# An attention, Fourier and MLP kernel: the MLP in thirds of a batch, with the residual added in place

## The chip, the cores and the metric

The kernel runs on one core of one Trainium2 chip. The metric is the device time of one execution in microseconds (us), with all inputs and outputs in HBM; runs of one kernel on one chip are compared with each other. Five engines work side by side, each through its own list of instructions in order: PE (matrix products), DVE (vector operations), ACT (activations and copies), POOL (a slower general engine) and SP (which here only issues DMAs). An instruction that waits holds up everything behind it on its own engine.

## What is computed

Four batches of 768 rows; q, k and v have 8 heads of 64, so a row has 512 values after attention. In numpy, cut to what matters:

```python
# attention: each chunk of 32 queries sees 16 keys to the left, its own 32, 8 to the right, 8 memory keys
a = np.exp(scale * q_c @ k_full.T - max); a = a / a.sum()
x[:, chunk] = a @ v_full                       # then heads side by side: (4, 768, 512)

mixed = np.real(np.fft.fft(np.fft.fft(x, axis=1), axis=2))
u = x + mixed
un = (u - u.mean(-1)) / np.sqrt(u.var(-1) + 1e-06)
ch = np.maximum(un @ w_ch1, 0.0) @ w_ch2       # 512 -> 2048 -> 512
return u + ch                                  # (4, 768, 512) float32
```

The last three lines are where the change lies: layer 1 (`w_ch1`) with its ReLU, layer 2 (`w_ch2`), and the residual `u`.

## The kernel before

**Rows and tiles.** A batch is six tiles of 128 rows. `xs[b]` (tile `xsb`, 128x6x512 float32, three buffers for four batches) holds a batch from the end of its attention on: first `x`, later `u`, written over it.

**Attention.** Heads go in pairs; pair n (0 to 15, four for each batch) loads q and k by POOL's DMAs and v by SP's (`e_load_v`, L350: seven DMAs, two of 220 KB among them, into buffer `va` n mod 4, so pair n + 4 loads into the buffer that pair n reads). PE turns q and k (batch 3's are turned by SP's DMAs instead), makes scores (`sc`), ACT takes their exponentials (`e`), PE multiplies them with the values (`xa`, `xo`, L455), and DVE divides into `xs[b]` (L465, L466).

**Fourier.** DVE folds the rows (`zy`, `pq`, `ff`), splits them into a high and a low half in 16 bits (`hi` by ACT, `lo` by DVE), PE multiplies by sine and cosine tables (`ps`, 193 columns wide), ACT and DVE split the result (`up`), and PE multiplies along the other axis (`e_columns`, L695: eight matmuls with 256 moving columns, each with its own stationary operand). The lower three tiles of a batch are got from the upper ones, with rows mirrored through HBM (`x_rows`, `x_back`, `xr`).

**Normalisation.** Tile by tile, in the order 0, 1, 3, 4, 2, 5 (batch 0: 0 to 5), DVE makes `u` (L701 or L585), its statistics (L709, L710), and ACT writes `un` = mean - u in float16 (L715). The scale by the deviation is left to the end, since ReLU lets a positive factor through. Then `un` is turned into `unT`: by PE and a DVE copy in batch 0, and in batches 1 to 3 by a DMA transpose from SP's queue, `e_flip` (L724), called a flip below. `SLOT` gives a tile its place in `unT`: places 0 to 5 hold tiles 0, 3, 4, 5, 1, 2.

**MLP.** `mlp` (L1172) takes a half of a batch at a time, 384 rows (three places). Layer 1 is 16 groups (`e_ch1`, L752) of four matmuls with 384 moving columns; after each, ACT's ReLU (`e_relu`, L759) writes a 128x384 slice of `hT`. Layer 2 (`e_ch2`, L766) makes each tile of 128 rows by 16 matmuls with 512 moving columns; DVE multiplies by `rstd` and adds `u` into a new tile `osb` (L795, four buffers), and a DMA stores `osb`: directly, or for mirrored rows by way of HBM (`out_rows`). The last tile of batch 3 goes in two halves of 256 columns (L773, L779, L787).

**What sets the order.** The class `Plan` simulates the engines with costs written in the code and emits the instructions in the order that comes out. The MLP's matmuls have the lowest rank: PE takes them when nothing else is ready in the plan. In its rows, `take` and `give` are buffers that a step needs and frees. Once the program is built the order is fixed, and each engine waits at its next instruction. PSUM has four banks (`mlp`, `acc`) that layer 1, layer 2, the Fourier products and the second half of the values share.

Of the kernel before, what the change touches and what calls it, by code (L numbers as in the profile page):

```python
# [177 lines left out]
def kernel(  # L178
# [47 lines left out]
    def let_go(t):  # L226
        for name, held in bank_of.items():
            for h in held:
                if h[0] is t:
# [15 lines left out]
    TURNED = 3  # L245
    cp_q = "p h j d -> p h (j d)"
# [4 lines left out]
                     xsb=3, fold=2, hl=1, up=4, dn=1, acc=2, mlp=2, un=6, unT=2, hT=1, osb=4))  # L251
# [5 lines left out]
    mkf = fpool.tile([P, 2, D], FP32, tag="osb", bufs=4, name="mkf")  # L257
    mkb = fpool.tile([P, 2 * D], BF16, tag="osb", bufs=4, name="mkb")
# [5 lines left out]
    yS = fpool.tile([P, 3, 2, NK], FP32, tag="unT", bufs=2, name="yS")  # L264
    rS = fpool.tile([P, 3, 2, NK], FP32, tag="unT", bufs=2, name="rS")
# [4 lines left out]
    ident = fpool.tile([P, P], FP32, tag="osb", bufs=4, name="ident")  # L270
# [204 lines left out]
    mu_of, unT_of, rstd_of, g_of = {}, {}, {}, {}  # L475
# [115 lines left out]
    def g_zy(par, g):  # L591
        if g == 0:
            zy_of[0, par] = fpool.tile([P, NST, P], FP32, tag="unT", bufs=2, name="zy0")
        xb, sl = xs[0], slice(3 * g, 3 * g + 3)
        nc.vector.tensor_tensor(zy_of[0, par][:, sl], xb[:, sl, 0:P], xb[:, sl, HD:HD + P],
                                ALU.add if par == 0 else ALU.subtract)
# [115 lines left out]
    def e_un(b, kt):  # L712
        un_of[b, kt] = un = fpool.tile([P, DM], FP16, tag="un", bufs=6, name="un")

        nc.scalar.activation(un, xs[b][:, kt, :], AFT.Identity, bias=mu_of[b][:, kt, 0:1],  # L715
                             scale=-1.0)
# [6 lines left out]

    def e_flip(b, kt):  # L724
        if kt == 0:
            unT_of[b] = fpool.tile([P, NDT, S], FP16, tag="unT", bufs=2, name="unT")
        nc.sync.dma_start_transpose(unT_of[b][:, :, ts(SLOT.index(kt), P)], un_of.pop((b, kt)))

    def e_unT(b, kt):
        if kt == 0:  # L730
            unT_of[b] = fpool.tile([P, NDT, S], FP16, tag="unT", bufs=2, name="unT")
        tp = tp_of.pop((b, kt))
        nc.vector.tensor_copy(unT_of[b][:, :, ts(kt, P)], tp)
        let_go(tp)

    def e_rstd(b):
        rstd_of[b] = rstd = fpool.tile([P, NST], FP32, tag="rstd", bufs=2, name="rstd")
        nc.gpsimd.tensor_scalar(rstd, mu_of[b][:, :, 1], eps, None, ALU.add)
        nc.gpsimd.tensor_tensor(rstd, rstd, mhalf, ALU.pow)

# [9 lines left out]
    ph_of, pc_of, hT_of, osb_of = ({} for _ in range(4))  # L750

    def e_ch1(b, sh, ht):  # L752
        ph_of[b, sh, ht] = ph = bank(pick(b, sh, ht)["tag"], [P, 512], FP32, "ph")
        for dt in range(NDT):
            nc.tensor.matmul(ph[:, 0:384], w1_sb[:, dt, ts(ht, P)],  # L755
                             unT_of[b][:, dt, sh * 384:(sh + 1) * 384],
                             start=(dt == 0), stop=(dt == NDT - 1))

    def e_relu(b, sh, ht):  # L759
        if ht == 0:  # L760
            hT_of[b, sh] = fpool.tile([P, NHT, 384], FP16, tag="hT", bufs=1, name="hT")
        ph = ph_of.pop((b, sh, ht))
        nc.scalar.activation(hT_of[b, sh][:, ht, :], ph[:, 0:384], AFT.Relu, bias=0.0, scale=-1.0)  # L763
        let_go(ph)

    def e_ch2(b, sh, stl, part):  # L766
        if part == 0:
            pc_of[b, sh, stl] = bank(pick(b, sh, stl, 0)["tag"], [P, DM], FP32, "pc")
        for ht in range(4 * part, 4 * part + 4):
            nc.tensor.matmul(pc_of[b, sh, stl], hT_of[b, sh][:, ht, ts(stl, P)], w2_sb[:, ht, :],  # L770
                             start=(ht == 0), stop=(ht == NHT - 1))

    def e_ch2_half(b, sh, stl, half):  # L773
        pc_of[b, sh, stl, half] = pc = bank(pick(b, sh, stl, 1 + half)["tag"], [P, HD], FP32, "pc")
        for ht in range(NHT):
            nc.tensor.matmul(pc, hT_of[b, sh][:, ht, ts(stl, P)], w2_sb[:, ht, ts(half, HD)],
                             start=(ht == 0), stop=(ht == NHT - 1))

    def e_osb_half(b, sh, stl, half):  # L779
        st, cols = slot(b, sh * 3 + stl), ts(half, HD)  # L780
        osb_of[b, st, half] = osb = fpool.tile([P, HD], FP32, tag="osb", bufs=4, name="osb")
        pc = pc_of.pop((b, sh, stl, half))
        nc.vector.scalar_tensor_tensor(osb, pc, rstd_of[b][:, st:st + 1], xs[b][:, st, cols],
                                       ALU.mult, ALU.add)
        let_go(pc)

    def e_out_half(b, st, half):  # L787
        (nc.sync, nc.scalar)[half].dma_start(out[b, ts(st, P), ts(half, HD)],
                                             osb_of.pop((b, st, half)))

    def e_osb(b, sh, stl):
        st = slot(b, sh * 3 + stl)
        osb_of[b, st] = osb = fpool.tile([P, DM], FP32, tag="osb", bufs=4, name="osb")
        pc = pc_of.pop((b, sh, stl))
        nc.vector.scalar_tensor_tensor(osb, pc, rstd_of[b][:, st:st + 1], xs[b][:, st, :],  # L795
                                       ALU.mult, ALU.add)
        let_go(pc)

    def e_out(b, st):
        (nc.scalar if b == B - 1 else nc.sync).dma_start(out[b, ts(st, P), :], osb_of.pop((b, st)))  # L800

    def e_out_rows(b, st):
        nc.sync.dma_start(od[b % 2, st - 3], osb_of.pop((b, st)))
# [200 lines left out]
    def weights(n):  # L1004
# [5 lines left out]
        else:  # L1010
            t_w2.extend(add("POOL", 0.7, lambda g=g: nc.gpsimd.dma_start(
                w2_sb[:, ts(g, 4), :], w2v[:, ts(g, 4), :]), moved=2.6, late=2.0,
                behind=t_ck[n], rank=t_ck[n]["rank"] + 0.1) for g in range(4))

    def first_fourier():
        t_rest, t_mid, t_row, pre = {}, {}, {}, {}
        for g in range(2):
            for par in range(2):
                zy = add("DVE", 0.5, lambda par=par, g=g: g_zy(par, g),
                         [t_norm[0, g], t_norm[1, g], t_sines],  # L1020
                         take=("unT",) if g == 0 else ())
# [7 lines left out]
                for ab in range(2):  # L1029
# [3 lines left out]
                                          take=("fold",) if (ab, g) == (0, 0) else (),  # L1033
                                          give=("unT",) if (ab, g) == (1, 1) else ())
# [12 lines left out]
            for par in range(2):  # L1047
                for ab in range(2):
# [5 lines left out]
                    else:  # L1054
                        ff = add("DVE", 0.55, lambda par=par, ab=ab: g_both(par, ab),
                                 pre[par, ab, 1][:2], give=("unT",) if ab == 1 else ())
# [59 lines left out]
    def columns_of(b, t_rest):  # L1116
        t_dn, t_un, cols = {}, {}, {}
        allr = list(t_rest.values())
        kts, sa = (0, 1, 2, 3, 4, 5), None
        if b == 0:  # L1120
# [21 lines left out]
        for i, kt in enumerate(kts):  # L1142
# [12 lines left out]
            sa = add("DVE", 0.9, lambda kt=kt: e_stats(b, kt), [su, sa])  # L1155
            un = add("ACT", 0.72, lambda kt=kt: e_un(b, kt), [sa], take=("un",))
            if b > 0:
                t_un[kt] = add("SP", 1.2, lambda kt=kt: e_flip(b, kt),
                               [un], behind=t_un.get(kts[i - 1]) if i else None,
                               take=("unT",) if i == 0 else (), give=("un",), late=2.5,  # L1160
                               loose=True)
                continue
# [3 lines left out]
                           take=("unT",) if kt == 0 else (), give=("mlp",))  # L1166
        rs = add("POOL", 1.0, lambda: e_rstd(b), [sa])
        return t_un, rs

    mlp_prev = [None]  # L1170

    def mlp(b, t_un, rs):  # L1172
        for sh in range(2):
            relu = []
            c2 = None
            for ht in range(NHT):
                ph = add("PE", 0.65, lambda sh=sh, ht=ht: e_ch1(b, sh, ht),
                         mlp_prev + [t_un[slot(b, 3 * sh + i)] for i in range(3)] + t_w1,
                         pick=pick(b, sh, ht), give=("unT",) if sh == 1 and ht == NHT - 1 else (),
                         rank=MLPS + len(plan.tasks), filler=True)  # L1180
                relu.append(add("ACT", 0.5, lambda sh=sh, ht=ht: e_relu(b, sh, ht),
                                [ph, relu[-1] if relu else None],
                                take=("hT",) if ht == 0 else (), give=(pick(b, sh, ht),),
                                rank=RELU(len(plan.tasks))))
            for stl in range(3):
                st, end_b = slot(b, 3 * sh + stl), 3 * sh + stl == NST - 1
                if end_b and b == B - 1:
                    for half in range(2):
                        c2 = add("PE", 1.76, lambda sh=sh, stl=stl, half=half:
                                 e_ch2_half(b, sh, stl, half), [relu[-1], t_w2[3], c2],  # L1190
                                 pick=pick(b, sh, stl, 1 + half), rank=MLPS + len(plan.tasks))
                        os_ = add("DVE", 0.4, lambda sh=sh, stl=stl, half=half:
                                  e_osb_half(b, sh, stl, half), [c2, rs], take=("osb",),
                                  give=(pick(b, sh, stl, 1 + half),))
                        add(("SP", "ACT")[half], 0.5, lambda st=st, half=half:
                            e_out_half(b, st, half), [os_], give=("osb",), moved=0.5)
                    continue
# [71 lines left out]
```

## Time and profile before

| What | Value |
|---|---|
| three timed runs | 284.81, 285.5, 283.14 us; median 284.81 |
| profiled execution, its own time from first to last instruction | span 284.2 us; the page gives nothing outside the span |
| granted PE clock | 1.000 |
| layer 1 matmul, 128x384, x512 | 86.7 us busy, 326 ns each (pipelined: the next starts before it ends) |
| layer 2 matmul, 128x512, x368 | 85.4 us busy, 380 ns each |
| ReLU on ACT, 128x384, x128 | 61.1 us busy, 492 ns each |
| `un` on ACT, 128x512, x24 | 17.3 us busy, 719 ns each |
| residual on DVE, 128x512, x23 | 17.2 us busy, 749 ns each |
| PE idle for the flip of batch 1 (`ph` waits for `unT`) | 1.5 us, once |

Busy times of PE overlap, so the time that a group of matmuls takes is read from the starts of consecutive groups, not from the mean of one. "L755" is line 755 of the kernel before; `ph` is layer 1's PSUM tile, `pc` layer 2's, `pm` that of `e_columns`.

### The profile page before, as it was taken

How to read it: one execution, taken by the hardware profiler on the slowest of the kernel's cores; microseconds unless marked ns; L12 is line 12 of the kernel's file. 1: busy time of each engine (PE TensorE's matmuls, PEld its weight loads, DVE VectorE, ACT ScalarE, POOL GpSimd, SP SyncE). 2: the span in 40 equal slices, each digit the busy share in tenths (PEclk: the TensorE clock that was granted, in tenths of full speed). 3: DMA queues.
4: the chain of work that ended last, by engine and by line, in shares of the span. 5: the costliest groups of instructions: out<-in, count | busy, mean ns of one | idle time of the engine just before them, and what ended most of it. 6: DMA issues, size and time to landing. Idle time of an engine off the chain costs nothing.

```text
span 284.2 us, 7142 instructions
## 1 busy us (share of the span) xinstructions
PE 267.9 (94%) x2941; PEld 170.7 (60%) x2941; DVE 164.4 (58%) x348; ACT 158.6 (56%) x294; POOL 58.3 (21%) x107
## 2 busy tenths in 40 slices
PE   0599999999999999998999999999999999999994
PEld 0476798765666766655667555657665545645644
DVE  7968979960348973897886960497669112012012
ACT  6887666588576575655952387228424822712700
POOL 8842652240210093441001020010000200000000
PEclk9999999999999999999999999999999999999999
DMA  6999999999899999999989963339304534004204
GB/s 102 202 168 167 194 204 204 197 197 192 134 199 271 145 233 156 140 155 211 154 180 113 205 158 64 78 149 148 113 0 111 140 83 110 4 37 111 39 37 111
DMA packets 116112, 39.92 MB, mean 140 GB/s; under 512 B 104560, under 2 KB 111472, under 8 KB 116080
## 3 DMA queue, kind: packets, MB, share of 16 engines
q1 hardware_dynamic: 93888, 23.54, 47.1%
q0 software_dynamic: 21472, 15.21, 34.0%
q10 hardware_dynamic: 720, 0.72, 0.8%
q8 instruction: 23, 0.38, 0.6%
q14 instruction: 9, 0.07, 0.1%
HBM read 37.36 MB, written 13.37 MB: 178 GB/s over the span
## 4 chain that ended last, share of the span: by engine, by line
PE 81%; DMA 11%; DVE 3%; SPq 1%; issue 1%; ACT 0%; POOL 0%; POOLq 0%; DVEq 0%
PE ph L755 30%; PE pc L770 27%; PE ps L527 6%; DMA va<-in_v_dram 5%; PE pm L695 4%; PE xa L455 3%; PE ps L684 3%; PE xo L455 3%; DMA va<-in_mem_v_dram 2%; PE sc L431 2%; DMA qs<-in_q_dram 2%; DMA unT<-un 2%; PE trq L375 1%; PE trk L375 1%; DVE xsb L701 1%; DVE st L709 1%
## 5 line engine op out<-in xcount | busy, mean ns | idle before, releaser
L755 PE MATMUL ph<-unT,w_sb 128*128 128x384 f16 x512 | 86.7, 326 | 1.5 <-DMA unT<-un 1.5
L763 ACT ACTIVATE hT<-ph 128x384 f16<-128x384 f32 x128 | 61.1, 492 | 47.8 <-PE ph L755 46.4
L770 PE MATMUL pc<-w_sb,hT 128*128 128x512 f16 x368 | 85.4, 380 | 0.0
L755 PEld LDWEIGHTS <-w_sb 128*128 128x128 f16 x512 | 49.2, 98 | 33.9 <-issue 1.9
L770 PEld LDWEIGHTS <-hT 128*128 128x128 f16 x368 | 34.1, 98 | 38.0 <-issue 0.7
L795 DVE SCALAR_TENSOR_TENSOR osb<-pc,rstd,xsb 128x512 f32<-128x512 f32 x23 | 17.2, 749 | 63.7 <-PE pc L770 63.7
L439 ACT ACTIVATE e<-sc,mbias 128x384 f32<-128x384 f32 x64 | 33.6, 577 | 16.2 <-PE sc L431 16.2
L715 ACT ACTIVATE un<-xsb,mu_s 128x512 f16<-128x512 f32 x24 | 17.3, 719 | 17.8 <-DVE mu_s L710 17.7
L539 ACT CAST up<-ps 128x386 f16<-128x386 f32 x16 | 9.6, 602 | 16.0 <-PE ps L527 15.5
L709 DVE BATCH_NORM_STATS2 st<-xsb 128x6 f32<-128x512 f32 x24 | 16.5, 689 | 0.6
L544 DVE TENSOR_TENSOR up<-ps,up 128x386 f16<-128x386 f32 x16 | 9.6, 600 | 11.6 <-ACT up L539 11.4
L517 DVE TENSOR_TENSOR lo<-ff,hi 128x768 f16<-128x768 f32 x12 | 11.5, 958 | 8.0 <-ACT hi L512 7.8
L455 PE MATMUL xa<-va,e 128*64 128x65 f32 x384 | 15.4, 232 | 0.0
L455 PEld LDWEIGHTS xa<-va,e 128*64 128x64 f32 x384 | 13.2, 143 | 3.4 <-issue 2.6
L455 PE MATMUL xo<-va,e 128*64 128x65 f32 x384 | 14.1, 223 | 0.0
L431 PEld LDWEIGHTS <-kTb 64*128 64x128 bf16 x384 | 7.8, 97 | 9.0 <-issue 7.3
L393 ACT COPY qT<-trq 128x768 bf16<-128x768 bf16 x12 | 9.5, 793 | 6.3 <-PE trq L375 6.3
L455 PEld LDWEIGHTS xo<-va,e 128*64 128x64 f32 x384 | 12.6, 138 | 0.4 <-ACT kTb L406 0.3
L570 POOL DMA_DIRECT2D xr<-x_back x3 | 2.3, 768 | 50.7 <-DMA x_back<-x_rows 50.7
L431 PE MATMUL sc<-qT,kTb 64*128 64x64 bf16 x384 | 11.5, 195 | 0.7 <-POOL va L315 0.6
L701 DVE TENSOR_TENSOR xsb<-pm,xsb 128x512 f32<-128x512 f32 x15 | 10.1, 674 | 3.5 <-PE pm L695 3.4
L347 POOL DMA_DIRECT2D qs<-in_q_dram x12 | 8.0, 669 | 19.0 <-PE xa L455 10.6
(153 smaller groups left out, 361.8 us busy)
## 6 DMA issues: line engine op xcount, KB each, us to landing
va<-in_v_dram SPq DMA_DIRECT2D x32, 220.0 KB
w_sb<-in_moe_w_ch_dram POOLq DMA_DIRECT2D x8, 512.0 KB, 16.3
out_dram<-osb SPq DMA_DIRECT2D x12, 256.0 KB
qs<-in_q_dram POOLq DMA_DIRECT2D x12, 192.0 KB, 6.8
ks<-in_k_dram POOLq DMA_DIRECT2D x12, 192.0 KB, 7.6
x_rows<-xsb POOLq DMA_DIRECT2D x3, 768.0 KB, 5.5
xr<-x_back POOLq DMA_DIRECT2D x3, 768.0 KB, 5.8
out_rows<-osb SPq DMA_DIRECT2D x9, 256.0 KB
```

Source lines behind the costliest of these rows:

```text
L431: nc.tensor.matmul(sc[:, hh, t6, :], kT[r0:r0 + 64, t, :], qT[r0:r0 + 64, ts(t, 64)], start=True, stop=True, tile_position=(r0, 0))
L439: nc.scalar.activation(e1[:, :, :, ts(half, 32)], sc[:, :, 0:6, ts(half, 32)], AFT.Exp, bias=mbias[:, half:half + 1], scale=1.0 / math.sqr ...
L455: nc.tensor.matmul(xa[64 * half:64 * half + 64, st, hh, 0:65], e1[:, hh, t6, :], v1[:, hh, 6 * g + t6, 0:65], start=True, stop=True)
L517: nc.vector.tensor_tensor(lo[:, ab].rearrange(fl), ff_of[b, par][:, ab].rearrange(fl), hi[:, ab].rearrange(fl), ALU.subtract)
L527: nc.tensor.matmul(out_[:, sp, :], part[:, ab, sp * 3 + st, c0:c1], tab[:, sp, st, :], start=(st == 0 and i == 0), stop=(st == 2 and i == 1))
L701: nc.vector.tensor_tensor(uv, pm_of[b, kt], uv, ALU.add)
L709: nc.vector.bn_stats(st6, xs[b][:, kt, :])
L715: nc.scalar.activation(un, xs[b][:, kt, :], AFT.Identity, bias=mu_of[b][:, kt, 0:1], scale=-1.0)
L755: nc.tensor.matmul(ph[:, 0:384], w1_sb[:, dt, ts(ht, P)], unT_of[b][:, dt, sh * 384:(sh + 1) * 384], start=(dt == 0), stop=(dt == NDT - 1))
L763: nc.scalar.activation(hT_of[b, sh][:, ht, :], ph[:, 0:384], AFT.Relu, bias=0.0, scale=-1.0)
L770: nc.tensor.matmul(pc_of[b, sh, stl], hT_of[b, sh][:, ht, ts(stl, P)], w2_sb[:, ht, :], start=(ht == 0), stop=(ht == NHT - 1))
L795: nc.vector.scalar_tensor_tensor(osb, pc, rstd_of[b][:, st:st + 1], xs[b][:, st, :], ALU.mult, ALU.add)
```

## The change

A unit of the MLP is now a third of a batch, two places, 256 rows: tiles 0 and 3, then 4 and 5, then 1 and 2 (batch 0: 0 and 1, 2 and 3, 4 and 5). Layer 1 makes two of the 16 groups, i and i + 8, in one bank, by eight matmuls with 256 moving columns, and one ReLU of 128x512 takes both. Layer 2 still makes one tile of 128 rows by 16 matmuls of 512 columns. The residual is added into `xs[b]` itself, and the stores go from there; so batch 3 may take batch 0's buffer of `xs` only when batch 0's last store is done. `osb` is gone, and the last tile is no longer cut in two. `unT` is held in five thirds instead of two whole batches. In batch 0 layer 1 runs for two thirds before their layer 2; the second third's `hT` has a buffer of its own. The tables `yS`, `rS`, `zy0`, `ident` and `mkf` use other buffers, and the four parts of `w_ch2` are loaded in the order 0, 2, 1, 3.

The diff also brings functions for another way to make layer 2 (`e_w2t`, `e_s`, `e_prod`, `e_add`, `e_scale`); they run only for units that the list `FAST` names, and it is empty.

```diff
+    FAST = []
+    EVEN = {b for b, j in FAST}
...
-                     xsb=3, fold=2, hl=1, up=4, dn=1, acc=2, mlp=2, un=6, unT=2, hT=1, osb=4))
+                     xsb=3, fold=2, hl=1, up=4, dn=1, acc=2, mlp=2, un=6, unT=5, hT=1, S=1))
...
+    def unT(b, kt):
+        i = kt if b == 0 else SLOT.index(kt)
+        if (b, i // 2) not in unT_of:
+            unT_of[b, i // 2] = fpool.tile([P, NDT, 2 * P], FP16, tag="unT", bufs=5, name="unT")
+        return unT_of[b, i // 2][:, :, ts(i % 2, P)]
...
-        nc.sync.dma_start_transpose(unT_of[b][:, :, ts(SLOT.index(kt), P)], un_of.pop((b, kt)))
+        nc.sync.dma_start_transpose(unT(b, kt), un_of.pop((b, kt)))
...
-            nc.tensor.matmul(ph[:, 0:384], w1_sb[:, dt, ts(ht, P)],
-                             unT_of[b][:, dt, sh * 384:(sh + 1) * 384],
-                             start=(dt == 0), stop=(dt == NDT - 1))
+        for k in range(2):
+            for dt in range(NDT):
+                nc.tensor.matmul(ph[:, k, :], w1_sb[:, dt, ts(HH * k + i, P)], unT_of[b, j][:, dt, :],
+                                 start=(dt == 0), stop=(dt == NDT - 1))
...
-        nc.scalar.activation(hT_of[b, sh][:, ht, :], ph[:, 0:384], AFT.Relu, bias=0.0, scale=-1.0)
+        nc.scalar.activation(hT_of[b, j][:, :, i, :], ph, AFT.Relu, bias=0.0,
+                             scale=1.0 if b in EVEN else -1.0)
...
+            nc.vector.scalar_tensor_tensor(u, pc, rstd_of[b][:, st:st + 1], u, ALU.mult, ALU.add)
...
-        (nc.scalar if b == B - 1 else nc.sync).dma_start(out[b, ts(st, P), :], osb_of.pop((b, st)))
+        (nc.scalar if b == B - 1 else nc.sync).dma_start(out[b, ts(st, P), :], xs[b][:, st, :])
...
-        nc.sync.dma_start(od[b % 2, st - 3], osb_of.pop((b, st)))
+        nc.sync.dma_start(od[b % 2, st - 3], xs[b][:, st, :])
...
-                               take=("unT",) if i == 0 else (), give=("un",), late=2.5,
-                               loose=True)
+                t_un[kt] = add("SP", 1.2, lambda kt=kt: e_flip(b, kt), [un],
+                               behind=t_un.get(kts[i - 1]) if i else None,
+                               take=room(kt), give=("un",), late=2.5, loose=True)
...
+        for i in range(HH):
+            ph = add("PE", 0.875, lambda i=i: e_ch1(b, j, i),
+                     mlp_prev + [t_un[t] for t in tiles] + t_w1, pick=pick(b, j, i),
+                     give=("unT",) if i == HH - 1 else (), rank=MLPS + len(plan.tasks), filler=True)
+            relu.append(add("ACT", 0.6, lambda i=i: e_relu(b, j, i),
+                            [ph, relu[-1] if relu else None],
...
     def mlp(b, t_un, rs):
+        if b == 0:
+            relu = [layer1(0, 0, t_un), layer1(0, 1, t_un)]
+            for j in range(2):
+                layer2(0, j, relu[j], rs)
+        for j in range(2 if b == 0 else 0, 3):
+            layer2(b, j, layer1(b, j, t_un), rs)
```

## The prediction

> **What bounds the kernel now.** I read the page's busy shares first, then its chain of waits by engine.
>
> ```profile
> PE 267.9 (94%) x2941; PEld 170.7 (60%) x2941; DVE 164.4 (58%) x348; ACT 158.6 (56%) x294; POOL 58.3 (21%) x107
> ...
> PE 81%; DMA 11%; DVE 3%; SPq 1%; issue 1%; ACT 0%; POOL 0%; POOLq 0%; DVEq 0%
> ```
>
> PE is busy for 94% and carries 81% of the chain; 10 of its idle 16 us lie before 20 us. So the time is PE's work plus the places where PE waits. The chain in order of time shows both: at each line the start, the length, and what ran.
>
> ```profile
> 123.82 4.90 DMA unT<-un
> 128.73 0.14 issue
> 128.86 6.66 PE ph L755 x40
> ...
> 209.60 1.75 PE pm L695 x16
> ...
> 218.25 10.40 PE ph L755 x64
> 228.65 10.36 PE pc L770 x48
> ...
> 270.17 6.92 PE pc L770 x32
> 277.12 0.76 DVE osb L795
> 277.90 2.69 DMA out_dram<-osb
> ```
>
> From 218.25 on PE runs MLP alone, without gaps. Before that there is one stall worth naming: at 128.86 layer 1 of batch 1 begins, and PE had nothing to do for 1.46 us, since the third flip that it needs (tile 4's) landed late. The third view is SP's timeline, since flips stand in SP's list.
>
> ```profile
> 101.22 1.17 SPq L360 DMA_DIRECT2D va<-in_v_dram  x1
> ...
> 117.88 1.28 SPq L727 DMA_TRANSPOSE unT<-un  x1
> 119.27 1.33 SPq L384 DMA_TRANSPOSE kU<-ks  x1
> 120.69 5.67 SPq L727 DMA_TRANSPOSE unT<-un  x4
> ...
> 136.45 0.59 SPq L360 DMA_DIRECT2D va<-in_v_dram  x1
> 137.14 1.02 SPq L356 DMA_DIRECT2D va<-in_v_dram  x2
> 138.22 0.30 SPq L365 DMA_DIRECT2D va<-in_mem_v_dram  x1
> 138.62 2.98 SPq L356 DMA_DIRECT2D va<-in_v_dram  x2
> 141.64 0.31 SPq L365 DMA_DIRECT2D va<-in_mem_v_dram  x1
> ```
>
> A flip holds SP for 1.2 us. The last five lines are one pair's seven value loads (pair 15's): 5.5 us of SP's time, well behind the flips. From 74 us on, other pairs' seven took 3.4 (from 97.23), 4.8, 5.0, 5.2, 5.7 and at most 8.2 us (from 101.22, beside POOL's loads of q and k).
>
> **PE's work.** By the chain, 64 matmuls of 384 columns take 10.40 us (162.5 ns each), 32 of 512 take 6.92 (216 ns), 16 of 256 with new weights each take 1.75 (109 ns). Layer 1: 512 x 162.5 = 83.2 us becomes 768 x 109 = 83.7, +0.5. Layer 2: 368 x 216 + 32 x 109 = 83.0 becomes 384 x 216 = 82.9, no change. Where a group of full-width matmuls follows one of the small ones (scores, turns, values), its first costs 0.11 more in the chain (eight `ph` 1.41 for 1.30, four `pc` 0.97 for 0.86). Counted in the order in which the two programs' instructions stand, from the first layer 1 on, such places go from 30 to 32, +0.2; the `xa` groups that follow a small group directly, 0.71 us instead of 0.85, go from two to none, +0.3. Together +1.0 us, all on the path.
>
> [...] The rows of this trace (162.5, 109, 216) follow the number of columns, and I go by them.
>
> **ReLU, residual, stores.** 128 ReLUs of 492 ns become 96 of 128x512. No row shows one; in proportion to the columns it is 656 ns, and the `un` row of that size gives 719. Eight matmuls before it take 0.87 us, so either is hidden behind PE, and ACT's sum stays at about 61 us (96 x 656 = 63). With one free bank only, PE would wait for the ReLU; the banks are tight while batch 1's Fourier products run (about 100 to 118 us). DVE's last `lo` before them has, by my count of DVE's rows, some 0.8 us to spare. I put 0.2 us for both, between 0 and 1.5. The residual keeps its form and 749 ns. Batch 3 may write `xs` only when batch 0's last stores are done: they follow PE's layer 2 at about 127 us and land by about 135, and batch 3's first values come after 150, so 15 us cover it.
>
> **The tail.** Before, PE ends at 280.6 and the span at 284.2: 3.6 us for half a residual (0.48) and half a store. After, it is a whole residual (0.75) and a whole store; the row of such a store is 2.69 us, the half one took 2.97. So 3.5 to 3.8; +0.1.
>
> **The stall before batch 1.** This decides. Two places instead of three must be ready: the flips of tiles 0 and 3, one fewer. But the plan moves SP's list: tile 0's flip, then pair 15's seven value loads, then the flips of tiles 1, 3, 4, 2, 5. The loads write the buffer that pair 11's values are read from, so SP stands still there until PE has made those, and the flips queue behind it.
>
> PE: before, the groups from 56.92 to layer 1 of batch 1 add up to 69.5 us, and the trace has 70.5 (127.4, without the stall); the 0.96 are small waits that the sum lacks. After, the groups add up to 70.3, so PE is there at 56.9 + 70.3 + 0.96 = 128.1. Pair 11's values end, by the same sum, at 119.3. SP: 119.3, seven loads 5.2 us (the middle of the rows), tile 1's flip 1.2, so tile 3's begins at 125.7 (its `un`, about 121, is no bound). From the start of a flip to its landing the trace has 5.5 us (tile 4's, 123.2 to 128.7) and 4.2 (the q flip at 115.15, whose reader goes on at 119.33); with 4.9 it is there at 130.6. The stall is 2.5 us in place of 1.46. Bounds: loads 3.4 and landing 4.2 give 0; loads 8.2 and landing 5.5 give 6.1. I take the middle, since SP's load around 119 is neither alone nor at its worst (pair 14's loads and POOL's q and k run just before).
>
> That a flip behind the loads waits for their packets too is not in any row. [...]
>
> **The other units.** Layer 1 of (1,1) needs tile 5 at 144 us, its flip is out by 131. Batch 2's first unit now comes 16.1 us after its first `pm`, since the MLP runs further ahead of the attention; tile 3's flip begins about 9.8 us after that `pm` (sum, statistics and pair 13's two divisions on DVE, then `un`) and lands by 14.0 to 15.3. Covered by 0.8 to 2.1; behind the mirrored stores on SP's queue it could cost up to 2 us; I take 0.2. Batch 3's first unit has 15.4 us for 12.5.
>
> **The sum.** +1.0 (PE) - 1.46 + 2.5 (stall) + 0.1 (tail) + 0.2 (banks, DVE) + 0.2 (batch 2) = +2.5. The profiled execution's 284.2 us becomes 286.7; its span is 0.6 under the median of the runs, 284.81, which becomes 287.3.
>
> **Rivals.**
>
> *The flips come in time.* If the seven loads take 3.4 us as the row at 97.23 did, the stall goes: 284.8 + 1.0 - 1.5 + 0.5, hence 284.8, no change or a shade faster. For it: DMA traffic is lower in some stretches. Against: only one of seven such loads was that short.
>
> *The value loads jam SP.* They take 8.2 us as from 101.22, and the flips land at 5.5: stall 6.1, and 284.8 + 1.0 - 1.5 + 6.1 + 0.5 = 290.9, slower. It decides from a stall of 2.85 us on, that is loads of over 5.55 us with a landing of 4.9. For it: DMA engines are busiest just there (share 1.62 from 112 to 128 us).
>
> *Weight loads bind at 256 columns.* A weight load's row is 98 ns, under 109, so only if loading `w_sb` for 256 columns went slower than loading `up` does. With 10 ns more a matmul +7.7 us, 295. Against: the last half tile, 32 matmuls of 256 columns, took 3.59 us for its loads, 112 ns each, like `pm`.
>
> *The change doesn't do what it says*: it does; only the second way of layer 2 is not run, and costs nothing.
>
> **How the numbers follow.** My forecast, a stall of 1 to 4 us: 0.55, and 287.3 is its middle. In time: 0.2. Jam: 0.2. Weight loads: 0.05. Of runs of this kernel about 1% (2.85 us) can be told from no change. The forecast spreads from 285.8 to 288.8, so about 0.18 of its 0.55 lie over 287.66; with jam (0.2) and weight loads (0.05) slower is 0.43. Faster by 1% would need 2.85 us off a PE that has 1.46 us of stall to give: 0.04. Same: 0.53. The range takes the low case whole (284.4) and reaches to the jam (291.0); outside remain the weight loads and a jam with a second stall in batch 2.
>
> **What would show it.** Right: 768 matmuls of 256 columns, 64 in 7.0 us in the last stretch; a wait of PE's `ph` for the flip of batch 1, near 128 us, and in SP's timeline value loads between the first and the second flip of that batch; ReLUs of 0.6 to 0.7 us. Wrong: no wait there, a wait at batch 2's first unit (near 172 us), or groups of 64 at over 7.2 us.

## The result, and the profile after

| | before | after |
|---|---|---|
| median of the timed runs | 284.36 us (283.14 to 285.5, 4 runs) | 293.28 us (292.77 to 294.13, 4 runs) |
| ratio to before | | 1.0315, 95% interval 1.0274 to 1.0356: slower |
| profiled execution, span | 284.2 us | 292.0 us |
| granted PE clock, mean | 1.000 | 0.988 |

The time lies over the predicted range, which ended at 291.0. A timed run is about 1.7 us longer than its span, in all runs that list both, so the two medians stand for spans of some 282.7 and 291.6 us. Line numbers below are those of the changed kernel (layer 1 is L775, layer 2 L793, the flips L748, the value loads L358 to L367), and of the kernel before where its runs are shown.

First the page of the changed kernel: the busy line, PE's share and its clock in 40 slices, the chain's shares, and two of the costliest groups.

```profile
PE 271.3 (93%) x3181; PEld 195.6 (67%) x3181; DVE 163.9 (56%) x347; ACT 154.1 (53%) x262; POOL 60.0 (21%) x107
...
PE   0599999999999999947999999999999999999994
...
PEclk9999999999999999995999999999999999999999
...
PE 86%; POOL 5%; DMA 3%; DVE 2%; SPq 1%; issue 1%; POOLq 0%
...
L775 PE MATMUL ph<-unT,w_sb 128*128 128x256 f16 x768 | 92.7, 277 | 5.9 <-DMA unT<-un 5.9
L784 ACT ACTIVATE hT<-ph 128x512 f16<-128x512 f32 x96 | 57.0, 598 | 72.0 <-PE ph L775 71.6
```

Layer 1 and ReLU have the new forms, and the ReLU's 598 ns are hidden behind PE. One place stands out: PE is idle in the 18th and 19th slice (digits 4 and 7), and in the 19th the clock falls to 5 tenths. All 5.9 us that layer 1 waited for a flip are one wait. The chain in order of time shows it, and the last stretch beside it:

```profile
127.18 1.22 SPq L748
...
128.50 4.55 DMA unT<-un
133.05 0.14 issue
133.19 9.70 PE ph L775 x64
...
274.07 6.99 PE ph L775 x64
```

The same 64 matmuls take 6.99 us at 274.07 and 9.70 at 133.19, right behind the wait. Busy time by stretches gives the reason; the columns are the stretch, its length, the busy time of PE, PEld, DVE, ACT and POOL with the number of instructions, the granted clock, the DMA share and GB/s.

```profile
124.00:128.00 4.00, 3.26 (x16) 1.27 (x13) 3.79 (x9) 0.72 (x1) 1.67 (x3) 1.00 1.07 165
128.00:131.50 3.50, 0.00 (x0) 0.00 (x0) 3.46 (x7) 0.00 (x0) 3.41 (x3) 1.00 2.13 146
131.50:133.20 1.70, 0.01 (x1) 0.04 (x2) 1.24 (x2) 0.00 (x0) 0.32 (x1) 0.54 1.35 203
133.20:138.40 5.20, 5.20 (x25) 3.61 (x26) 0.00 (x0) 1.19 (x2) 0.00 (x0) 0.50 1.28 219
138.40:142.90 4.50, 4.50 (x42) 3.93 (x41) 1.25 (x2) 3.54 (x6) 1.68 (x2) 0.99 1.04 215
```

PE stops at 127.27. The clock stays at 1.00 until about 131.6, falls to 0.50, and is back at about 138.4, so 25 matmuls run at half speed. Why the flip was late stands in SP's timeline:

```profile
112.42 0.59 SPq L362 DMA_DIRECT2D va<-in_v_dram  x1
113.33 1.72 SPq L358 DMA_DIRECT2D va<-in_v_dram  x2
115.10 0.30 SPq L367 DMA_DIRECT2D va<-in_mem_v_dram  x1
116.09 3.37 SPq L358 DMA_DIRECT2D va<-in_v_dram  x2
119.50 0.31 SPq L367 DMA_DIRECT2D va<-in_mem_v_dram  x1
119.99 2.19 SPq L382 DMA_TRANSPOSE qT<-qs  x1
122.28 1.20 SPq L748 DMA_TRANSPOSE unT<-un  x1
123.58 0.61 SPq L362 DMA_DIRECT2D va<-in_v_dram  x1
...
127.18 7.55 SPq L748 DMA_TRANSPOSE unT<-un  x5
```

Pair 14's seven loads and pair 12's q flip hold SP until 122.18; then come tile 0's flip, pair 15's seven loads from 123.58 to 127.08, and the other five flips. The third in the row, tile 3's, begins at 128.45 and lands at 133.05. Its `un` had been written by 120.8. In the kernel before, pair 14's loads too stood behind these flips, so the plan moved two pairs' loads ahead, not one. Their first line before:

```profile
131.54 1.56 SPq L360 DMA_DIRECT2D va<-in_v_dram  x1
```

The two profiles differ by 7.8 us. The wait gives 5.92 - 1.46 = 4.46, the clock 9.70 - 6.99 = 2.71, the tail behind PE's last matmul 0.4 (4.0 for 3.6), PE's own work 0.68 (PE's end less the start of the first layer 1, less wait and clock: 287.98 - 56.47 - 5.92 - 2.71 = 222.88, before 280.6 - 56.92 - 1.46 = 222.2), and the first layer 1 starts 0.45 earlier. That adds up to 7.8.

### The profile page after: what moved, and what is told of

It reads as the page before. It is cut to its first block, busy times and chain, and to the rows that moved or that the text cites. A ratio compares the mean times of both kernels' runs of the same rounds, so it can differ in the third digit from the quotient of the medians.

```text
span 292.0 us, 7576 instructions
## 1 busy us (share of the span) xinstructions
PE 271.3 (93%) x3181; PEld 195.6 (67%) x3181; DVE 163.9 (56%) x347; ACT 154.1 (53%) x262; POOL 60.0 (21%) x107
## 4 chain that ended last, share of the span: by engine, by line
PE 86%; POOL 5%; DMA 3%; DVE 2%; SPq 1%; issue 1%; POOLq 0%
PE ph L775 30%; PE pc L793 28%; PE ps L529 5%; PE xa L457 4%; PE xo L457 4%; PE pm L699 3%; PE ps L688 3%; PE sc L433 3%; DMA qs<-in_q_dram 2%; DMA unT<-un 2%; PE idle L902 1%; PE trk L377 1%; PE trq L377 1%; DVE xsb L705 1%; PE pm L580 1%
## 5 line engine op out<-in xcount | busy, mean ns | idle before, releaser
L775 PE MATMUL ph<-unT,w_sb 128*128 128x256 f16 x768 | 92.7, 277 | 5.9 <-DMA unT<-un 5.9
L784 ACT ACTIVATE hT<-ph 128x512 f16<-128x512 f32 x96 | 57.0, 598 | 72.0 <-PE ph L775 71.6
L793 PE MATMUL pc<-w_sb,hT 128*128 128x512 f16 x384 | 87.6, 379 | 0.0
L775 PEld LDWEIGHTS <-w_sb 128*128 128x128 f16 x768 | 74.3, 99 | 19.3 <-DVE zy L489 6.4
L793 PEld LDWEIGHTS <-hT 128*128 128x128 f16 x384 | 36.4, 98 | 40.0 <-issue 0.3
L800 DVE SCALAR_TENSOR_TENSOR xsb<-pc,rstd,xsb 128x512 f32<-128x512 f32 x24 | 18.0, 748 | 65.2 <-PE pc L793 65.0
L467 DVE RECIPROCAL zs<-xa 128x6 f32<-128x6 f32 x16 | 3.0, 190 | 20.3 <-PE xa L457 20.3
```

The costliest lines, as they stand in the source:

```text
L775: nc.tensor.matmul(ph[:, k, :], w1_sb[:, dt, ts(HH * k + i, P)], unT_of[b, j][:, dt, :], start=(dt == 0), stop=(dt == NDT - 1))
L784: nc.scalar.activation(hT_of[b, j][:, :, i, :], ph, AFT.Relu, bias=0.0, scale=1.0 if b in EVEN else -1.0)
L793: nc.tensor.matmul(pc_of[b, j, r], hT_of[b, j][:, k, i, ts(r, P)], w2_sb[:, HH * k + i, :], start=(i + k == 0), stop=(i + k == HH))
L800: nc.vector.scalar_tensor_tensor(u, pc, rstd_of[b][:, st:st + 1], u, ALU.mult, ALU.add)
```

## The experiments

The theory: the order on SP's queue delays the flip, and the clock makes the delay dearer. The rivals: matmuls of 256 columns or thirds as such are slow, or `un` comes late.

**Pair 15's loads behind the flips.** The order that the plan gives is changed at one place before it is emitted:

```diff
-        for t in plan.order():
+        steps = plan.order()
+        held = [t_lv[15]]
+        steps = [t for t in steps if not any(t is h for h in held)]
+        at = next(i for i, t in enumerate(steps) if t is done[1][0][5])
+        steps[at + 1:at + 1] = held
+        for t in steps:
```

> The changed kernel with one step moved on SP alone: pair 15's seven value loads stand behind batch 1's six flips instead of between the first and the second. Theory (the flips queue on SP, PE idles, and its clock falls): tile 0's flip ends on SP at 123.5 as before, tile 1's at 124.7, tile 3's begins there and lands 4.6 us later, at 129.3; PE is there at 127.3, so the wait is 2.0 us instead of 5.92, and if 2 us do not cool the clock the 64 matmuls behind it take 7.0 instead of 9.70: span 292.0 - 3.9 - 2.7 = 285.4 (288.1 if they do). Rival A (256-column matmuls with more weight loads pull the clock down themselves): the wait shrinks but the slow stretch stays, 288.1. Rival B (DVE and ACT are late with un): the wait stays 5.9, 292.

Measured: 286.05 us (284.76 to 288.55, 10 runs), ratio 1.0068 [1.0035, 1.0102], span 286.5, clock 1.000. From its chain:

```profile
126.30 3.83 DMA unT<-un
130.13 0.14 issue
130.26 7.15 PE ph L775 x64
```

The wait is 2.7 us in place of 5.9, and the 64 matmuls behind it take 7.15. The profiled run took 288.22 us, 2.2 over the median; how long the wait was in the others isn't shown, and the longest (288.55) lists a clock of 0.993. Moving seven DMA issues on one queue takes away about four fifths of the loss, with all the arithmetic of the thirds in place.

**All of batch 1's flips first.** As above, with `held = [t_lv[14], t_qf[12], t_lv[15]]` (pair 14's loads and pair 12's q flip too).

> As the run before, and pair 14's value loads and pair 12's q flip moved behind the flips too. Theory: each flip starts when its un is written (tile 3's at 120.8), tile 3's lands at about 125.4, before PE comes at 127.3: no wait at batch 1, no slow stretch, span 292.0 - 5.9 - 2.7 = 283.4, a little under the kernel before (284.2). Rival A: no wait, but 64 matmuls at over 7.2 us somewhere after 127, 286.1. Rival B: un is late, a wait of over 2 us stays.

Measured: 285.08 us (284.44 to 286.51, 10 runs), ratio 1.0026 [0.9999, 1.0053], span 283.7. SP's timeline, then the chain:

```profile
117.03 9.54 SPq L748 DMA_TRANSPOSE unT<-un  x6
126.66 0.61 SPq L362 DMA_DIRECT2D va<-in_v_dram  x1
```

```profile
120.75 6.91 PE pc L793 x32
127.65 6.99 PE ph L775 x64
```

Six flips in a row, and PE goes from layer 2 to layer 1 without a gap. So neither the thirds nor `un` cost the time: what is left of them is 0.26%, with an interval that reaches 1.000.

**PE kept busy through the wait.** The changed kernel's queue as it was, with 52 matmuls of a zero operand ahead of layer 1 of batch 1:

```diff
+    COLD = {(1, 0, 0): 52}
...
+        for _ in range(COLD.get((b, j, i), 0)):
+            nc.tensor.matmul(ph[:, 0, :], dz, strided(dz, 0, [[0, 2], [1, P]]), start=True, stop=True)
```

> The changed kernel with 52 more matmuls (zeros, 256 columns, 5.6 us) ahead of batch 1's layer 1, into the bank that its first group then starts anew; SP's order is as in the changed kernel. Theory: the flip lands at 133 as before, so layer 1 starts no earlier, but PE has not been idle, its 64 matmuls take 7.0 instead of 9.70: 292.0 - 2.7 = 289.3. Rival A (the clock falls from the kind of matmul): 9.7 stays, 292.

Measured: span 289.7, clock 0.998; 291.98 us (291.42 to 294.75, 4 runs), ratio 1.0297 [1.0226, 1.0369]. Chain:

```profile
127.33 6.07 DMA unT<-un
133.45 7.16 PE ph L778 x64
```

The flip is as late as in the changed kernel (127.33 + 6.07 = 133.40), and the 64 matmuls take 7.16 instead of 9.70: the profile shows the clock's part by itself, 2.5 us. The medians of the timed runs are only 1.3 us apart, and the two ratios' intervals overlap, so of the size in the timed runs they say little. The clocks that they list say that it fell in each run of the changed kernel: 0.986 to 0.988 in all four, by an estimate from these means 7 to 8 us at half speed, against 0.998 in three runs here and 0.994 in the fourth (294.75 us).

**Half as many dummies**, `COLD = {(1, 0, 0): 26}`, to see how long an idle time it takes.

> The changed kernel with 26 zero matmuls (2.8 us) on PE ahead of layer 1 of batch 1, half as many as e3_kept_warm. They fill the first half of the wait, some 3 us of idle time remain. If the clock falls only with a longer idle time than the 2.7 us of e1_load_behind, PE's clock stays at 1.00 and the 64 matmuls after it take 7.0 to 7.2 us: span 289.3, the same as with 52. If any idle time of 3 us is enough, they take 8 to 9.7 and the span is 290.5 to 292.0.

Measured: span 292.4, one run. The chain and the clock by stretches:

```profile
129.64 5.03 DMA unT<-un
134.72 8.57 PE ph L778 x64
```

```profile
126.00:130.00 4.00, 4.00 (x32) 3.02 (x31) 3.87 (x5) 0.00 (x0) 3.62 (x4) 1.00 1.62 185
130.00:134.00 4.00, 0.30 (x3) 0.02 (x1) 2.92 (x5) 0.00 (x0) 0.00 (x0) 1.00 1.13 260
134.00:138.00 4.00, 3.29 (x18) 2.41 (x19) 0.00 (x0) 0.60 (x1) 0.00 (x0) 0.57 0.67 142
```

The flip landed 1.6 us later than in the changed kernel's trace, so 4.4 us of idle time were left, not 3. After 4.4 us the clock falls and 1.6 are lost (8.57 for 6.99); in the profile of the first experiment, after 2.7, it doesn't.

**The kernel before without its own stall.** Before, k's flip of pair 12 stands ahead of three flips of batch 1; it is moved behind tile 2's (`held = [t_kf[12]]`).

> The kernel before (halves) with one step moved on SP: pair 12's k flip (1.33 us) stands behind tile 2's flip instead of behind tile 0's. Theory: the flips of tiles 1, 3, 4 go out 1.2 us earlier unless their un holds them (tile 4's un is written at 120.9), tile 4's lands at 127.5, and PE's wait of 1.46 us at batch 1 falls to 0.1 to 0.3: span 284.2 - 1.2 = 283.0. Rival (the landing is set by DMA traffic, not by SP's queue): 284.2.

Measured: no wait at batch 1, span 282.3; but 284.51 us (283.58 to 285.04, 10 runs), ratio 1.0001 [0.9974, 1.0028]. The stall that the prediction credited with 1.46 us is gone, and the timed runs don't show it. A second profile of the unchanged kernel asks whether it is there at all:

> The kernel before, unchanged, for a second profile. If its wait of 1.46 us for the flip at batch 1 is not in most executions, there is none here, and the span is 282.5 to 283 instead of 284.2; the term of -1.46 in the prediction then had nothing to take away. If the wait belongs to the kernel, it is 1 to 2 us again, with a span near 284.

Measured: 284.0 us, span 282.3, and among PE's waits:

```profile
PE ph L755 <- DMA unT<-un: 0.6, 1, 0.6
```

The stall changes from one execution to the next, 0.6 here. The profile shown before, with 284.2, lies near the upper end of what the kernel does: the 25 timed runs of before beside the first experiments have spans from 281.6 to 284.7. Against this second profile the changed kernel's is 9.7 us longer: 5.3 for the wait, 2.7 for the clock, 0.7 for PE's work, 0.5 for the tail, and 0.5 because its first layer 1 starts later.

**Halves with the loads first.** The opposite test: the kernel before, with pair 15's loads right behind tile 0's flip.

> The kernel before, in halves, with nothing changed but the place of pair 15's seven value loads on SP's queue: right after tile 0's flip, ahead of the other flips of batch 1, as the changed kernel has them. If the order on SP's queue is the cause: SP stands until pair 11's values have been read, then seven loads of 3.5 to 5 us, then k's flip and the flips of tiles 1, 3 and 4 (a half needs three), so tile 4's lands near 138 to 140; PE waits 10 to 13 us at layer 1 of batch 1, the clock falls there, and the first groups after it take 2 to 4 us longer: span 294 to 299, worse than the changed kernel. If the thirds are the cause (256 columns, places, banks), the kernel in halves bears that order well: span under 287, and a wait of 4 us at most.

Measured: 288.86 us (287.6 to 290.72, 4 runs), ratio 1.0145 [1.0100, 1.0191], span 287.4. It doesn't test the theory: in this order the loads stood ahead of pair 11's reads of the same buffer, so pair 11 is computed with pair 15's values, and SP had nothing to stand for (its loads began at 118.84). It does show something of the clock, since PE waited for these loads:

```profile
PE xa L455 <- DMA va<-in_mem_v_dram: 2.9, 1, 2.9
```

PE stopped at 125.87 and went on at 128.74; at 129.04 the clock fell to 0.50 all the same, and stayed there for 3.4 us; 40 matmuls of layer 1, from 131.80 on, take 6.97 us for 6.66. The four timed runs list clocks of 0.992, 1.000, 0.994 and 1.000, so with this program it fell in two of them and not in the other two. The next experiment puts the loads behind these reads, and k's flip, tiles 1, 3, 4 and 2 and pair 13's q flip behind the loads.

> The kernel before, in halves, with pair 15's value loads right after tile 0's flip on SP's queue, but behind pair 11's reads of that buffer (SP must stand until those are done, near 118.9 us); k's flip of pair 12 and the flips of tiles 1, 3, 4 and 2 come behind the loads, then q's of pair 13. If the order on SP's queue is the cause: loads 119 to 122.5 or 124, k's flip and tiles 1's and 3's to 126 or 128, tile 4's lands at 131 to 133; PE waits 4.5 to 6 us at layer 1 of batch 1, the clock falls, and the span is 288 to 291, as much over 282.3 as the changed kernel lost or somewhat less. If thirds are the cause (256 columns, places, banks), halves bear that order: span under 284.5.

Measured: 296.98 us (296.18 to 298.34, 4 runs), ratio 1.0449 [1.0400, 1.0498], span 294.6, clock 0.983. SP's timeline and the chain:

```profile
117.69 1.23 SPq L727 DMA_TRANSPOSE unT<-un  x1
125.70 0.63 SPq L360 DMA_DIRECT2D va<-in_v_dram  x1
...
129.74 1.25 SPq L384 DMA_TRANSPOSE kU<-ks  x1
131.09 5.14 SPq L727 DMA_TRANSPOSE unT<-un  x4
```

```profile
126.15 0.72 PE xo L455 x24
126.87 0.67 SPq L356
...
133.70 3.43 DMA unT<-un
137.13 0.14 issue
137.26 8.73 PE ph L755 x40
```

The expectation had taken pair 10's reads (near 118.9) for pair 11's, which end at 126.87; SP stands from 118.9 to 125.7. From there it runs as expected: loads, k's flip, three flips, tile 4's lands at 137.13, PE waits 10.4 us, and 40 matmuls of 384 columns take 8.73 instead of 6.66. So such a queue costs the kernel in halves 4.5%, without thirds and without matmuls of 256 columns in layer 1; the rival that thirds are the cause falls from this side too. Whether halves or thirds bear it better isn't shown: in the halves' plan pair 11's values are read 8.4 us later (to 126.87, against 118.50 in the changed kernel), and it is these that SP stands for.

**SP free as the prediction assumed.** The changed kernel with `held = [t_lv[14], t_qf[12]]`: pair 15's loads stay ahead of five flips, but SP is free when pair 11's values have been read.

> The changed kernel with pair 14's value loads and pair 12's q flip moved behind the six flips of batch 1 on SP's queue; pair 15's value loads stay ahead of five of them. SP then comes to these loads as soon as pair 11's values have been read (118.5 us in the changed kernel's trace), as the prediction had assumed. If the stall was mis-sized because SP came late: loads 118.5 to 122 or 123.7, tile 3's flip starts at 123.2 to 124.9 and lands at 127.4 to 129.5; PE waits 0 to 2.2 us, the clock stays at 1.00, span 283.7 to 286. If the loads ahead of the flips cost 5 us by themselves (by their packets, say), PE waits 4 us or more and the span is 288 or over.

Measured: 285.72 us (284.5 to 287.36, 10 runs), ratio 1.0043 [1.0015, 1.0071], span 284.1, clock 1.000. SP's timeline and the chain:

```profile
116.25 1.96 SPq L748 DMA_TRANSPOSE unT<-un  x1
118.30 0.61 SPq L362 DMA_DIRECT2D va<-in_v_dram  x1
...
123.00 0.31 SPq L367 DMA_DIRECT2D va<-in_mem_v_dram  x1
123.59 7.17 SPq L748 DMA_TRANSPOSE unT<-un  x5
```

```profile
124.92 2.79 DMA unT<-un
127.85 7.15 PE ph L775 x64
```

With SP there at 118.30 pair 15's loads ahead of the flips cost a wait of 1.0 us.

**A version that might beat both.** All flips first, and the last tile in two halves of 256 columns, as before:

```diff
+                if (b, j, r) == (B - 1, 2, 1):
+                    for half in range(2):
+                        c2 = add("PE", 1.76, lambda half=half: e_ch2_half(b, j, 1, half),
...
+                        os_ = add("DVE", 0.4, lambda half=half: e_res_half(b, j, 1, half), [c2, rs],
...
+                        add(("SP", "ACT")[half], 0.5, lambda half=half:
+                            e_out_half(b, tiles[1], half), [os_], moved=0.5)
+                    continue
```

> The changed kernel with all six flips of batch 1 ahead of the loads on SP's queue (as in e2_flips_first), and its last tile made in two halves of 256 columns again, as in the kernel before. If the rest of the loss is PE's work (+1.0 us) and a longer tail (4.0 us after PE's end instead of 3.6), the tail goes back to 3.6 and PE's end comes no later: span 283.3, 0.2 to 0.5 us under e2_flips_first, ratio to the kernel before 1.000 to 1.002. Rival: the halves cost as much on PE (16 more matmuls) as they spare at the end: 283.7, ratio 1.0026 as in e2_flips_first.

Measured: 284.57 us (284.01 to 285.2, 12 runs), ratio 0.9987 [0.9964, 1.0010], span 283.3; the tail behind PE's end is 3.4 us again, where all flips first had 4.0. It is as fast as the kernel before. No version was found that is faster.

## Why the prediction was wrong

It named the place, layer 1 of batch 1, and half of the cause, pair 15's loads ahead of the flips on SP. The other half is what stood ahead of those loads: pair 14's, 7.4 us on SP, and pair 12's q flip, 2.2. The experiments take the two apart:

| Ahead of tile 3's flip on SP | PE's wait in the profile, us | ratio of the timed runs |
|---|---|---|
| pair 14's loads with pair 12's q flip, and pair 15's loads (the changed kernel) | 5.92 | 1.0315 |
| pair 14's loads with the q flip | 2.7 | 1.0068 |
| pair 15's loads | 0.97 | 1.0043 |
| neither | none | 1.0026 |

The prediction's sign was right and its size about a third of what came; for "within 1%" it gave the larger chance. Of the 6.4 us between its +2.5 and the 8.9 between the medians, the profile gives 3.4 to the size of the stall and 2.7 to the clock. Step by step:

- **PE's work, +1.0.** Measured +0.68; with all flips first, PE's end less its first layer 1 is 279.74 - 56.86 = 222.88, again +0.7. 64 matmuls took 6.99 us, 109 ns each, as before (16 of `pm` in 1.75 us), and the rival of the weight loads falls.
- **The old stall, -1.46.** This was a credit read from one execution: the stall was 0.6 in the second profile, and taking it away changed the timed runs by nothing that could be measured. The prediction set the span of 284.2 against the median of 284.81 and found it 0.6 under; with the 1.7 us between a span and its time that profile was 1.1 over the median.
- **The new stall, +2.5.** This step failed. Its terms, as they stood, as the changed kernel ran, and with SP free:

| Term | predicted | after | SP free |
|---|---|---|---|
| SP comes to pair 15's loads | 119.3 | 123.58 | 118.30 |
| the seven loads take | 5.2 | 3.5 | 5.0 |
| tile 3's flip begins | 125.7 | 128.45 | 124.88 |
| begin to landing | 4.9 | 4.6 | 2.8 |
| PE is there | 128.1 | 127.27 | 126.88 |
| stall | 2.5 | 5.92 | 0.97 |

  The wrong term is the first: 119.3 was when the loads *may* start (pair 11's values read), taken for when SP *gets there*. SP's queue ahead of them was not summed: pair 14's loads to 119.81, the q flip of 2.19 and tile 0's flip of 1.20. The loads themselves, whose spread was to make the range, were short. One reading was wrong too, to no great effect: tile 4's flip before begins at 123.82, not 123.2, so begin to landing was 4.9 us and not 5.5, and the middle 4.55; that makes the stall 2.15, further from what came. The last column shows that with SP free the prediction's way of counting gives too much, not too little, and no loss of 3%.
- **The clock, 0.** This step is missing. It costs 2.71 us behind the wait, in the profile where the prediction had a bound for the stall of 6.1 (the rival of the jam, 290.9). The measured stall, 5.92, lies just under that bound, but by luck: the jam was to come from loads of 8.2 us, and they took 3.5. The profile of the kernel before had no row for it: its clock is listed as 1.00, also behind the wait of 1.46 us. The runs show a fall to 0.50 after 4.4, 5.9 and 10.4 us of idle time, and none in the profile with 2.7; with the loads first in halves the clock fell after 2.9 us. The least idle time after which it falls isn't shown.
- **Tail, +0.1.** Measured +0.4: with the residual's 0.75 us off, 3.2 us are left for the whole store, where the row of 2.69 was taken.
- **Banks, DVE and batch 2, +0.4.** No wait of these kinds: the only wait of layer 1 for a flip in the profile is that of batch 1.

What isn't settled is how much of the 8.9 us between the medians is the clock's. The profile says 2.7, the clocks of the timed runs say that it fell in each, but the timed runs with PE kept busy are only 1.3 us lower. The waits are also known from one profile of each program, two of the kernel before.

## What to carry to other kernels

When a change moves a DMA on a queue, add up the queue itself, every issue ahead of the one that matters with its own row, and take the later of "its data are ready" and "the queue gets there". Where PE may stand as long as it did here, add half-speed matmuls behind the wait to its price (in the profiles here the clock fell to 0.50 in PE's waits near layer 1 of batch 1 of 4.4, 5.9 and 10.4 us, and right behind one of 2.9, but not with one of 2.7). A stall seen in one profile is a credit only if a second profile shows it too.

## What the runs showed of the hardware

The four profiles in which the clock fell in a wait of PE near layer 1 of batch 1, or right behind it, in us:

| Run | PE's wait | clock falls after PE stops | clock at 0.50 for | of it PE at work | lost by the matmuls behind |
|---|---|---|---|---|---|
| halves, loads first | 2.9 | 3.2 | 3.4 | 2.8 | no row to compare |
| 26 dummies | 4.4 | 3.9 | 3.4 | 2.9 | 1.6 |
| the changed kernel | 5.9 | 4.3 | 6.8 | 5.3 | 2.7 |
| halves, loads behind the reads | 10.4 | 4.4 | 10.2 | 4.2 | 2.1 |

In these four rows the low stretches are once, once, twice and three times 3.4 us long. In the first row the clock fell when PE had been at work again for 0.3 us. In the other three rows, what is lost is about half of the time that PE works while the clock is low, so a longer wait need not cost more: 2.7 us behind 5.9, and 2.1 behind 10.4. What decides whether and for how long the clock falls isn't shown.

The time from a flip's begin on SP to its landing varied from 2.8 to 6.1 us across these runs, shortest and longest both with value loads ahead of it (2.8 with SP free, 6.1 with PE kept busy), and was 3.9 with pair 15's loads behind it. No rule could be read from them; that a flip lands later for the loads ahead of it in the queue, which the prediction found in no row, is neither shown nor refuted.
